# Gate and up products as pairs of 64-row matmuls on two row tiles, with the last 64 rows of K taken out of the seven products

## The chip, the cores and the metric

The kernel runs on one core of one Trainium2 chip. A core has five engines that run at the same time, each with its own queue of instructions worked off in order: TensorE (PE in the profile; its weight loads are listed apart as PEld), VectorE (DVE), ScalarE (ACT), GpSimd (POOL) and SyncE (SP), which here only issues transfers. Engines wait for each other by semaphores. Matrix products go to PSUM, eight banks of 128 partitions by 512 float32 values; everything else lives in SBUF, 128 partitions wide. The metric is device time in microseconds (us).

## The reference

`x` is 2048 tokens by 576 numbers. After a layer norm over the 576 numbers (`xn`), two branches are computed and joined.

```python
s = _A_ref(xn, A_wqkv, A_wo)     # linear attention, 32 heads of 18
def _B_ref(x, w_gate, w_up, w_down):          # B branch, 576 -> 4608 -> 576
    g = jnp.einsum("bsd,df->bsf", x, w_gate)
    u = jnp.einsum("bsd,df->bsf", x, w_up)
    h = _gelu(g) * u
    return jnp.einsum("bsf,fd->bsd", h, w_down)
return x + s * _silu(_B_ref(xn, B_w_gate, B_w_up, B_w_down))
```

The change touches the products by `w_gate` and `w_up`: 576 rows of K, 4608 columns each, 2048 tokens.

## The kernel before

**Words.** All large products are made in the type fp32r with each operand cut into two words: `hi` is the value rounded to fp32r, `lo` the rest. A product is then hi·hi + hi·lo + lo·hi, three matmuls over the same K. ScalarE writes `hi` (a copy), VectorE subtracts to get `lo`.

**Stages.** Normalization and the q, k, v products come first; the tokens turned to operands (`xo`, 128 rows by 5 slots by 512 tokens) are kept. The attention output follows (`s_mm`). Then comes the gate and up stage, 36 matrices of 256 columns (18 groups, each gate and then up), and after it the down products (`down_all`, PSUM tiles `bd`).

**Gate and up.** A Strassen-Winograd scheme works on a two by two split: K into two halves of 288 rows, the tokens into two halves again, the 256 columns of a matrix into two of 128. It needs seven products instead of eight. Each is made for two token sets of 512 (`SBS = (1, 0)`), so a product is two results of 128 columns by 512 tokens. Its left side is a weight block or a sum of blocks (A11, S2, S1, S3, A12, S4, A22, W_AT, line 855), its right side a token block or a difference (B11, T2, T1, T3, B21, B22, T4). The banks are `al`, `be`, `ga`, `de`, one of each for each set; `al`, `ga` and `de` are added to a second time by the fifth to the seventh product.

**One product** (`product`, line 907) is seven matmuls into one bank, by the table PASSES (line 54): 288 rows are two blocks of 128 and a rest of 32. Blocks 0 and 1 take three word pairs each. The seventh pass takes the three word pairs of the rest at once: the rest stands three times in slot 2, 32 rows each, so that 96 of 128 rows carry hi·hi, hi·lo and lo·hi. In all there are 7 products x 2 sets x 7 passes = 98 matmuls to a matrix.

**Around the products** (`matrix`, line 914): after each product VectorE or ScalarE takes its banks. `u` is a copy of `al` by ScalarE; sums with `be`, `ga`, `de` follow on VectorE; in a gate matrix ScalarE applies GELU to the four results as they come (`gate_matrix`, line 1025), in an up matrix VectorE multiplies into them (`up_matrix`, line 1045). The results stand in seventeen places (`spot_h`, `spot_m`, `spot_g`), are summed by GpSimd for the down stage and sent to DRAM (`hs`) by SP.

**The next matrix's weights** are prepared beside this: `load_mat` (line 862) loads the raw block into its one buffer `raw`, `mat_sums` (line 867) makes four block sums on GpSimd, `cut_w` (line 879) cuts words. `mat_pieces` (line 886) says after which product a piece goes: A11 after the first, S2, S1 and S3 after the fourth, A12 and A22 after the fifth, S4 after the sixth. They land in two tiles, `wa` and `wb`. After the last matrix's products stand pieces of the down stage in the same way (`down_first`, line 1306; `cut`, line 1126).

The program order on each engine is the order of the code (`tc.keep_in_program_order`); the waits are found by the framework from the tiles that are read and written.

Of the kernel before, what the change touches and what calls it, by code (L numbers as in the profile page):

```python
# [16 lines left out]
P = 128  # L17
S = 2048
D = 576
DF = 4608  # L20
# [71 lines left out]
SIGN = (-1, 1, -1, -1, 1, -1, 1, 1)  # L92

# [4 lines left out]
def block_kernel(ctx, tc, x, xe, xt, wq_d, wkv_d, wo, wgu_d, wd_d, out):  # L98
# [238 lines left out]
    def difference(s, i):  # L337
        f = xf[s]
        nm, a, b, o = SUMS[i]
        vec("tensor_sub", f[o], f[a], f[b])  # L340
        f[nm] = f[o]

    def keep(s, nm, o):
        d = dr.tile([P, 5, TBN], F32, name=f"kept_{s}_{nm}")
        dma(out=d, in_=o.bitcast(F32))
        store[s, nm] = d

    full = slice(0, TBN)

    def build(s, nm, i):  # L350
        xo[s][nm] = o = big(i, [P, 5, TBN], F32R, f"xo_{s}_{nm}")
        to_operand(o, xf[s][nm], full)
        return o
# [508 lines left out]
    def load_mat(q):  # L862
        if q < NQ:
            raw[q] = mid(0, [P, 2, 3, 2 * P], F32, f"raw_{q}")
            dma(out=raw[q], in_=wgu_d[q // 2, q % 2])

    def mat_sums(q):
        if q >= NQ:
            return
        rv = raw[q].rearrange("p j k (f c) -> p j f k c", f=2)  # L870
        a11, a21, a12, a22 = rv[:, 0, 0], rv[:, 0, 1], rv[:, 1, 0], rv[:, 1, 1]
        sm = mid(2, [P, 4, 3, P], F32, f"sm_{q}")
# [6 lines left out]
    def cut_w(o, src):  # L879

        r = slice(2 * KR, 3 * KR)
        act(o[:, :, 0:3, :], src, AF.Copy)
        vec("tensor_sub", o[:, :, 3:5, :], src[:, :, 0:2, :], o[:, :, 0:2, :].bitcast(F32))
        vec("tensor_sub", o[r, :, 2, :], src[r, :, 2, :], o[r, :, 2, :].bitcast(F32))

    def mat_pieces(q):
# [6 lines left out]
        else:  # L893
# [3 lines left out]
            ]  # L897
        return [
# [8 lines left out]
    def product(o, w, xop, start):  # L907
        for n, (wi, xi, rows) in enumerate(PASSES):
            nc.tensor.matmul(  # L909
                o, w[0:rows, wi, :], xop[0:rows, xi, :],  # L910
                start=(start and n == 0), stop=(n == len(PASSES) - 1), skip_group_check=True,
            )

    def matrix(q, c22, done, todo):

        u, bs = {}, {}

        def both(bk, wn, xn, start):
            for s in SBS:
                if start:  # L920
                    bs[bk, s] = (own_bank if bk == "al" else bank)(f"{bk}_{q}_{s}")
                product(bs[bk, s], w_at(q, wn), X[s][xn], start)

        both("al", "A11", "B11", True)
        for s in SBS:
            u[s] = tmp([P, TBN], f"u_{q}_{s}")
            act(u[s], bs["al", s], AF.Copy)
        run(todo[0])
        both("be", "S2", "T2", True)
        for s in SBS:  # L930
            vec("tensor_add", u[s], u[s], bs["be", s])
        run(todo[1])
        both("ga", "S1", "T1", True)
        for s in SBS:
            vec("tensor_add", c22(s), u[s], bs["ga", s])
        run(todo[2])
        both("de", "S3", "T3", True)
        for s in SBS:
            o = c22(s) if q % 2 == 0 else bs["be", s]
            vec("tensor_add", o, c22(s), bs["de", s])  # L940
            done(s, 1, 1, o)
        run(todo[3])
        both("al", "A12", "B21", False)
        for s in SBS:
            done(s, 0, 0, bs["al", s])
        run(todo[4])
        both("ga", "S4", "B22", False)
        for s in SBS:
            done(s, 0, 1, (u[s], bs["ga", s]))
        run(todo[5])  # L950
        both("de", "A22", "T4", False)
        for s in SBS:
            done(s, 1, 0, (u[s], bs["de", s]))
        run(todo[6])
# [579 lines left out]
    def form_begun(nm):  # L1534

        f = xf[0][nm]
        xo[0][nm] = o = big(12, [P, 5, TBN], F32R, f"xo_0_{nm}")
        act(o[:, 0:3], f, AF.Copy)

        def rest():  # L1540
            r = slice(KR, 2 * KR)
            vec("tensor_sub", o[:, 3:5], f[:, 0:2], o[:, 0:2].bitcast(F32))
# [177 lines left out]
```

## Time and profile before

| what | value |
|---|---|
| median of 3 runs | 1453.61 us (1453.46 to 1453.86) |
| profiled execution, its own time | 1452.58 us |
| span of its profile | 1450.9 us |
| TensorE busy, matmuls | 1444.4 us, 8272 matmuls |
| VectorE busy | 1148.7 us |
| ScalarE busy | 565.2 us |
| GpSimd busy | 580.1 us |
| gate and up stage | from 276.2 to 1076.0 us, 3528 matmuls |

The span is what the profile covers; 1.7 us of the profiled execution lie outside it. Busy time of an engine is the union of its instructions; a matmul's recorded length contains its way through the array, so one matmul's record overlaps the next, and the pace is read from the distance of starts, or from the length of a stretch over the number of its matmuls. In the lines by group the numbers are: count, busy time, mean length of one in ns, idle time of the engine just before them.

### The profile page before, as it was taken

How to read it: one execution, taken by the hardware profiler on the slowest of the kernel's cores; microseconds unless marked ns; L12 is line 12 of the kernel's file. 1: busy time of each engine (PE TensorE's matmuls, PEld its weight loads, DVE VectorE, ACT ScalarE, POOL GpSimd, SP SyncE). 2: the span in 40 equal slices, each digit the busy share in tenths (PEclk: the TensorE clock that was granted, in tenths of full speed). 3: DMA queues.
4: the chain of work that ended last, by engine and by line, in shares of the span. 5: the costliest groups of instructions: out<-in, count | busy, mean ns of one | idle time of the engine just before them, and what ended most of it. 6: DMA issues, size and time to landing. Idle time of an engine off the chain costs nothing.

```text
span 1450.9 us, 22169 instructions
## 1 busy us (share of the span) xinstructions
PE 1444.4 (100%) x8272; PEld 1286.5 (89%) x8272; DVE 1148.7 (79%) x1609; ACT 565.2 (39%) x918; POOL 580.1 (40%) x520
## 2 busy tenths in 40 slices
PE   9999999999999999999999999999999999999998
PEld 8989989988888888888888888888889999999998
DVE  7688666476787887887777878778888978989898
ACT  6444365333222233322332232332235556555454
POOL 3342340225756567566475754667632000000000
PEclk9999999999999999999999999999999999999999
DMA  5554115521532315224242243323379888767886
GB/s 221 186 205 158 45 36 207 224 95 51 171 101 100 131 52 188 88 95 140 72 159 87 97 150 102 117 87 121 126 272 347 269 261 252 249 188 235 278 293 225
DMA packets 119253, 235.04 MB, mean 162 GB/s; under 512 B 11658, under 2 KB 45354, under 8 KB 117226
## 3 DMA queue, kind: packets, MB, share of 16 engines
q1 hardware_dynamic: 116346, 221.37, 45.4%
q0 software_dynamic: 2656, 12.06, 2.2%
q8 instruction: 65, 1.06, 0.3%
q14 instruction: 42, 0.34, 0.1%
q10 hardware_dynamic: 144, 0.20, 0.0%
HBM read 150.96 MB, written 82.58 MB: 161 GB/s over the span
## 4 chain that ended last, share of the span: by engine, by line
PE 97%; DVE 1%; ACT 1%; issue 0%; POOL 0%; DVEq 0%; ACTq 0%; POOLq 0%
PE bd L147 25%; PE al L909 16%; PE ga L909 16%; PE de L909 16%; PE kv L147 8%; PE be L909 8%; PE s L147 4%; PE q L147 3%; PE kv_a L147 1%; PE idle L147 0%; PE d L147 0%; PE kw L147 0%; PE b L147 0%; ACT e_q L141 0%; PE xt L264 0%
## 5 line engine op out<-in xcount | busy, mean ns | idle before, releaser
L150 POOL TENSOR_TENSOR sm<-raw 128x384 f32<-128x384 f32 x72 | 75.0, 1041 | 144.0 <-DMA raw<-in_wgu_dram 125.8
L147 PE MATMUL kv<-wkv,xo_B 128*128 128x412 f32 (+2 forms) x662 | 125.0, 347 | 0.3 <-ACT xo_B L141 0.3
L147 PEld LDWEIGHTS kv<-wkv,xo_B 128*128 128x128 f32 x662 | 120.2, 188 | 1.7 <-ACT xo_B L141 0.9
L144 DVE TENSOR_TENSOR wa<-sm,wa 128x768 fp32r<-128x768 f32 x72 | 90.5, 1257 | 36.0 <-ACT wa L141 35.2
L147 PE MATMUL bd<-w_head,hi 128*128 128x288 f32 x516 | 117.5, 294 | 0.0
L144 DVE TENSOR_TENSOR wb<-raw,wb 128x256 fp32r<-128x256 f32 (+1 forms) x108 | 103.2, 955 | 7.2 <-ACT wb L141 5.5
L144 DVE TENSOR_TENSOR wa<-raw,wa 128x256 fp32r<-128x256 f32 x72 | 66.8, 928 | 50.6 <-ACT wa L141 47.4
L141 ACT ACTIVATE hi<-raw_h 128x1024 fp32r<-128x1024 f32 x59 | 62.5, 1059 | 96.1 <-PE bd L147 55.7
L147 PE MATMUL bd<-w_end,hi 128*128 128x288 f32 x448 | 89.4, 294 | 0.0
L141 ACT ACTIVATE spot_h<-spot_h 128x512 f32<-128x512 f32 x49 | 30.7, 633 | 150.1 <-DVE spot_h L144 150.1
L147 PEld LDWEIGHTS bd<-w_head,hi 128*128 128x128 f32 x516 | 86.8, 188 | 0.1
L144 DVE TENSOR_TENSOR raw_h<-raw_h,hi 128x1024 fp32r<-128x1024 f32 x59 | 71.8, 1221 | 18.8 <-ACT hi L141 18.8
L141 ACT ACTIVATE wa<-sm 128x1152 fp32r<-128x1152 f32 x36 | 41.8, 1161 | 92.8 <-PE de L909 92.8
L147 PE MATMUL bd<-w_end,raw_h 128*128 128x288 f32 x264 | 77.6, 294 | 0.0
L141 ACT ACTIVATE u<-al 128x512 f32<-128x512 f32 x72 | 41.0, 592 | 90.0 <-PE al L909 60.0
L147 PEld LDWEIGHTS bd<-w_end,hi 128*128 128x128 f32 x448 | 71.6, 188 | 0.0
L147 PE MATMUL bd<-beside,raw_h 128*128 128x288 f32 x240 | 70.5, 294 | 0.0
L150 POOL TENSOR_TENSOR spot_h<-spot_h,spot_h 128x512 f32<-128x512 f32 x45 | 62.8, 1403 | 2.9 <-DVE spot_h L144 2.4
L909 PE MATMUL al<-xo_B,wa 128*128 128x512 f32 x252 | 63.0, 389 | 0.0
L909 PE MATMUL al<-xr_B,wa 128*128 128x512 f32 x252 | 63.0, 389 | 0.0
L909 PE MATMUL be<-xo_T,wa 128*128 128x512 f32 x252 | 63.0, 389 | 0.0
L909 PE MATMUL be<-xr_T,wa 128*128 128x512 f32 x252 | 63.0, 389 | 0.0
(278 smaller groups left out, 4036.8 us busy)
## 6 DMA issues: line engine op xcount, KB each, us to landing
raw_h<-hs SPq DMA_DIRECT2D x176, 256.0 KB
raw<-in_wgu_dram SPq DMA_DIRECT2D x36, 768.0 KB
hs<-spot_h SPq DMA_DIRECT2D x90, 256.0 KB
hs<-spot_g SPq DMA_DIRECT2D x80, 256.0 KB
b<-in_wd_dram SPq DMA_DIRECT2D x42, 432.0 KB
hs<-spot_m SPq DMA_DIRECT2D x38, 256.0 KB
raw_g<-hs SPq DMA_DIRECT2D x22, 256.0 KB
raw_a<-hs SPq DMA_DIRECT2D x20, 256.0 KB
```

Source lines behind the costliest of these rows:

```text
L141: pin(nc.scalar.activation(*args, **kw))
L144: pin(getattr(nc.vector, op)(*args, **kw))
L147: pin(nc.tensor.matmul(*args, **kw))
L150: pin(getattr(nc.gpsimd, op)(*args, **kw))
L909: nc.tensor.matmul(o, w[0:rows, wi, :], xop[0:rows, xi, :], start=(start and n == 0), stop=(n == len(PASSES) - 1), skip_group_check=True,)
```

## The change

The last 32 rows of each half of K, 64 rows in all, leave the Strassen scheme. The seven products then cover K as two halves of 256, six passes each (table MAIN: slots 0 and 1 are hi, 2 and 3 of the weight lo). The 64 rows are added to the four results directly: to C22 with the fourth product, to the others with the last three (`tail_of`).

Every pass is made of 64-row matmuls. The array's upper and lower 64 rows are two row tiles. A product now has two phases. In the first (`phase(False, ...)`) rows 0 to 63 of the weight meet token set 1 and rows 64 to 127 meet token set 0, matmul by matmul in turn, each into its set's bank. In the second (`phase(True, ...)`) the sets change rows. The two phases of a product do not follow each other: `step` puts the first phase of the next product between them. After each first phase ScalarE copies one column of set 0's bank to a small tile (`seen`). What followed a product before (`post_0` to `post_6`) now follows, in program order, the first phase of the product two further on.

The 64 rows stand in slot 2 of T1, T3 and T2 as hi in one half of the 128 rows and lo in the other, and as a fifth block of the raw weights, twice (rows 0 to 63 and again 64 to 127); `cut_tail` makes their hi and lo. One such matmul pair belongs to the first phase (hi weight, lo token) and two to the second (hi and lo weight, hi token). `cut_w` no longer cuts a third slot, GpSimd's sums are 256 wide instead of 384, a raw block is 5 x 256 values to a row instead of 6 x 256.

The core of the diff:

```diff
+MAIN = ((0, 0), (0, 2), (2, 0), (1, 1), (1, 3), (3, 1))
+XW = (0, 1, 3, 4)
+TAIL = {"T1": (0,), "T3": (1,), "T2": (0, 1)}
+TR = P // 2
...
     def difference(s, i):
...
-        vec("tensor_sub", f[o], f[a], f[b])
+        vec("tensor_sub", f[o][:, 0:2], f[a][:, 0:2], f[b][:, 0:2])
...
+    def tail(s, nm, o):
+        h = s * TR
+        for j in range(2):
+            vs = [xf[s][BS[b][j]][:, 2, :] for b in TAIL[nm]]
+            r, low = (slice(i + j * KR, i + (j + 1) * KR) for i in (h, TR - h))
+            v = vs[0][r]
+            if len(vs) == 2:
+                d = tmp([P, TBN], f"xd_{s}_{j}")
+                vec("tensor_sub", d[r], v, vs[1][r])
+                v = d[r]
+            act(o[r], v, AF.Copy)
+            vec("tensor_sub", o[low], v, o[r].bitcast(F32))
...
     def cut_w(o, src):
-        r = slice(2 * KR, 3 * KR)
-        act(o[:, :, 0:3, :], src, AF.Copy)
-        vec("tensor_sub", o[:, :, 3:5, :], src[:, :, 0:2, :], o[:, :, 0:2, :].bitcast(F32))
-        vec("tensor_sub", o[r, :, 2, :], src[r, :, 2, :], o[r, :, 2, :].bitcast(F32))
+        act(o[:, :, 0:2, :], src, AF.Copy)
+        vec("tensor_sub", o[:, :, 2:4, :], src, o[:, :, 0:2, :].bitcast(F32))
+
+    def cut_tail(q):
+        o, src = wt["tail", q % 2], raw[q][:, 4, :]
+        act(o[:, 0], src, AF.Copy)
+        vec("tensor_sub", o[:, 1], src, o[:, 0].bitcast(F32))
...
-    def product(o, w, xop, start):
-        for n, (wi, xi, rows) in enumerate(PASSES):
-            nc.tensor.matmul(
-                o, w[0:rows, wi, :], xop[0:rows, xi, :],
-                start=(start and n == 0), stop=(n == len(PASSES) - 1), skip_group_check=True,
-            )
+    def half_passes(rows, o, w, xop, tail_, late):
+        wi = [(w[rows, i, :], xop[rows, XW[k], :]) for i, k in MAIN]
+        if tail_:
+            wt_, xt_ = tail_
+            wi += [(wt_[rows, i, :], xt_[rows]) for i in range(1 + late)]
+        return [(o, a, b) for a, b in wi]
+
+    def phase(late, prod):
+        o, w, xs_, start, tails_ = prod["o"], prod["w"], prod["x"], prod["start"], prod["tail"]
+        pair = []
+        for rows, s in ((LOWER, 0 if late else 1), (UPPER, 1 if late else 0)):
+            pair.append([
+                (s, *p) for p in half_passes(rows, o[s], w, xs_[s], tails_ and tails_[s], late)
+            ])
+        n = len(pair[0])
+        for k in range(n):
+            for side in range(2):
+                s, o_, a, b = pair[side][k]
+                mm(
+                    o_, a, b, start=(start and not late and k == 0), stop=(late and k == n - 1),
+                    skip_group_check=True,
+                )
+
+    def step(prod, post):
+        phase(False, prod)
+        for s in TOUCH:
+            act(seen[:, s : s + 1], prod["o"][s][:, 0:1], AF.Copy)
+        for f in posts[:-1]:
+            f()
+        del posts[:-1]
+        for p in begun_:
+            phase(True, p)
+        begun_[:] = [prod]
+        posts.append(post)
...
+        both("al", "A11", "B11", True, post_0)
+        both("be", "S2", "T2", True, post_1)
+        both("ga", "S1", "T1", True, post_2)
+        both("de", "S3", "T3", True, post_3, tail_of(1, "T3"))
+        both("al", "A12", "B21", False, post_4, tail_of(0, "T1"))
+        both("ga", "S4", "B22", False, post_5, tail_of(0, "T3"))
+        both("de", "A22", "T4", False, post_6, tail_of(1, "T2"))
```

How the change moves instructions is shown at two places. The first is TensorE at the start of matrix 10 (a gate matrix). A name such as `al_10_1` is the bank, the matrix and the token set; `xo_1_B11` and `xr_B11` are block B11 of set 1 and of set 0. Before, seven passes of one set follow each other:

```order
L909 MATMUL al_10_1_4674<-xo_1_B11_1135,wa_2927 128x512 x7
L909 MATMUL al_10_0_4682<-xr_B11_2594,wa_2927 128x512 x7
L909 MATMUL be_10_1_4698<-xo_1_T2_2544,wa_2927 128x512 x7
L909 MATMUL be_10_0_4706<-xr_T2_2686,wa_2927 128x512 x7
L909 MATMUL ga_10_1_4718<-xo_1_T1_2335,wa_2927 128x512 x7
```

Now, with only the first pair of each phase shown (each is repeated five times, and `de_9` has two pairs from the tail behind):

```order
L152 MATMUL al_10_1_5656<-xo_1_B11_1151,wa_2953 128x512 [waits DVE_49]
L152 MATMUL al_10_0_5657<-xr_B11_2621,wa_2953 128x512 [waits DVE_49]
L152 MATMUL de_9_0_5505<-xr_T4_3075,wb_3060 128x512 [waits Activation_49]
L152 MATMUL de_9_1_5504<-xo_1_T4_2709,wb_3060 128x512
L152 MATMUL be_10_1_5693<-xo_1_T2_2564,wa_2953 128x512
L152 MATMUL be_10_0_5694<-xr_T2_2712,wa_2953 128x512
L152 MATMUL al_10_0_5657<-xr_B11_2621,wa_2953 128x512 [waits Activation_49]
L152 MATMUL al_10_1_5656<-xo_1_B11_1151,wa_2953 128x512
```

The two sets alternate matmul by matmul, the second phase of a product stands behind the first phase of the next, and it begins with a wait for ScalarE. The second place is ScalarE from the end of matrix 10 into matrix 11. Before:

```order
L141 ACTIVATE wb_3036<-raw_11_4626 128x384 [waits Activation_49]
L141 ACTIVATE wb_3036<-raw_11_4626 128x384
L141 ACTIVATE spot_h0_3053<-spot_h0_3053 128x512 [waits DVE_49]
L141 ACTIVATE spot_g4_3062<-spot_g4_3062 128x512 [waits DVE_49]
L141 ACTIVATE wb_3036<-sm_11_4669 128x384 [waits PE_49,Activation_49,Pool_49]
L141 ACTIVATE spot_h2_3055<-spot_h2_3055 128x512 [waits DVE_49]
L141 ACTIVATE spot_g0_3058<-spot_g0_3058 128x512 [waits DVE_49]
L141 ACTIVATE u_11_1_4853<-al_11_1_4837 128x512 [waits PE_49]
```

Now:

```order
L146 ACTIVATE wb_3060<-raw_11_5632 128x256 x3
L146 ACTIVATE seen_87<-al_11_0_5919 128x1 [waits PE_49,Activation_49]
L146 ACTIVATE spot_h0_3077<-spot_h0_3077 128x512 [waits DVE_49]
L146 ACTIVATE spot_g4_3086<-spot_g4_3086 128x512 [waits DVE_49]
L146 ACTIVATE wb_3060<-sm_11_5651 128x256 [waits Pool_49]
L146 ACTIVATE seen_87<-be_11_0_5956 128x1 [waits PE_49,Activation_49]
L146 ACTIVATE spot_h2_3079<-spot_h2_3079 128x512 [waits DVE_49]
L146 ACTIVATE spot_g0_3082<-spot_g0_3082 128x512 [waits DVE_49]
L146 ACTIVATE seen_87<-ga_11_0_5987 128x1 [waits PE_49,Activation_49]
```

The one-column copies of matrix 11's first phases now stand between the GELUs of matrix 10's last two products (`spot_...<-spot_...`), and TensorE's second phases wait for these copies.

More of the change, by code (lines that the diff above doesn't have):

```diff
@@ L914, in matrix, with flush @@
+    begun_, posts = [], []
+    def step(prod, post):
[9 more added lines that the diff above has]
+        posts.append(post)
+    def flush():
+        phase(True, begun_.pop())
+        for f in posts:
+            f()
+        posts.clear()
     def matrix(q, c22, done, todo):
@@ L932, in matrix @@
[L932 to L954, printed above, removed]
+        wtail = wt["tail", q % 2]
+        def tail_of(f, nm):
+            c = slice(f * P, (f + 1) * P)
+            return [(wtail[:, :, c], X[s][nm][:, 2, :]) for s in range(2)]
+        def both(bk, wn, xn, start, post, tail_=None):
+            if start:
+                for s in SBS:
+                    bs[bk, s] = (own_bank if bk == "al" else bank)(f"{bk}_{q}_{s}")
+            step({
+                "o": [bs[bk, s] for s in range(2)], "w": w_at(q, wn), "start": start,
+                "x": [X[s][xn] for s in range(2)], "tail": tail_,
+            }, post)
```

125 lines of the change are left out of this document (88 added, 37 removed).

## The prediction

> **What bounds the kernel now.** I read the page first: busy times, then the chain that ended last.
>
> ```profile
> PE 1444.4 (100%) x8272; PEld 1286.5 (89%) x8272; DVE 1148.7 (79%) x1609; ACT 565.2 (39%) x918; POOL 580.1 (40%) x520
> PE 97%; DVE 1%; ACT 1%; issue 0%; POOL 0%; DVEq 0%; ACTq 0%; POOLq 0%
> ```
>
> TensorE is busy over the whole span and makes 97% of the chain. The waits of PE, all of them, say that nothing holds it up:
>
> ```profile
> PE idle L147 <- POOL ident masks.py:199: 1.6, 1, 1.6
> PE kv L147 <- ACT xo_B L141: 0.3, 1, 0.3
> PE bd L147 <- DVE raw_h L144: 0.2, 1, 0.2
> ```
>
> So time can only come from fewer or quicker passes, and any wait that the change adds to PE is paid in full. The stretch of the gate and up matmuls (duration, then PE busy with its count, PEld, clock, DMA), and below it the whole stage before it:
>
> ```profile
> 276.20:1076.00 799.80, 799.67 (x3528) 662.11 (x3528) 1.00 0.35 119
> 0.00:276.00 276.00, 273.94 (x1934) 254.31 (x1935) 196.52 (x400) 134.97 (x296) 85.11 (x112) 1.00 0.42 150
> ```
>
> 799.80 / 3528 = 0.2267 us a pass, at the full clock (1.00), 98 passes and 22.2 us a matrix. The timeline shows the same pace: seven passes start 1.59 us before the next seven.
>
> ```profile
> 633.38 1.75 PE L909 MATMUL al<-xr_B,wa 128*128 128x512 f32 x7
> 634.97 1.75 PE L909 MATMUL be<-xo_T,wa 128*128 128x512 f32 x7
> ```
>
> **The count.** Three products have 12 main pairs, four have 12 and three tail pairs: 84 + 12 = 96 pairs a matrix against 98 passes. Matmuls and weight loads rise from 98 to 192. All hangs on the time T of a pair: the stage takes 36 x 96 x T = 3456 T. It breaks even at 799.8 / 3456 = 0.2314.
>
> **What a pair costs.** No row of the trace shows two row tiles at once. The nearest are column tiles: `d` makes four matmuls of 128 columns beside each other, `xt` is one such matmul after another.
>
> ```profile
> 196.82 0.32 PE L147 MATMUL d<-ph,small 128*32 128x128 f32 x4
> 196.82 1.08 PE L147 MATMUL d<-ph,small 128*32 128x128 f32 x32
> 7.19 0.85 PE L264 MATMUL xt<-ident,x 128*128 128x128 f32 x6
> L147 PEld LDWEIGHTS d<-ph,small 128*32 128x32 f32 x160 | 4.1, 110 | 0.8 <-issue 0.8
> L147 PEld LDWEIGHTS kv_a<-pk,va 128*64 128x64 f32 x256 | 8.8, 135 | 2.7 <-issue 2.1 <-POOL va L150 0.3 <-ACT va L141 0.2
> L909 PEld LDWEIGHTS al<-xo_B,wb 128*128 128x128 f32 x252 | 47.3, 188 | 9.8
> 29.21 0.14 PEld L147 LDWEIGHTS kv_a<-pk,va 128*64 128x64 f32 x2 [0.28 <-issue]
> ```
>
> Four start within 0.32 - 0.275 = some 0.03 us (7 ns or so apart). Eight groups of four last 1.08: with 0.27 for the last group, seven steps of about 0.11 us. `xt` alone: (0.85 - 0.27) / 5, about 0.12. So a group of four costs what one costs, and the skew between tiles is hidden. Row tiles as good as that give T = 0.227. I take this value.
>
> From below: a pass of 288 columns in the down stage,
>
> ```profile
> 1199.96 0.29 PE L147 MATMUL bd<-w_end,raw_h 128*128 128x288 f32 x1
> 1200.09 0.43 PE L147 MATMUL bd<-w_end,beside 128*128 128x288 f32 x2
> 1200.35 0.29 PE L147 MATMUL bd<-w_end,raw_h 128*128 128x288 f32 x1
> 1200.48 0.29 PE L147 MATMUL bd<-w_end,beside 128*128 128x288 f32 x1
> ```
>
> four starts in 0.52, 0.130 each. Then 224 columns cost 0.097, or 0.43 ns each, and 512 columns 0.221. The remaining 6 ns and the uncertainty of the slope (0.41 ns would make it 0.21) are what pairs could hide: T from 0.21.
>
> From above: two 128-column weight loads belong to each pair. If they go one after the other, `bd` bounds them: one load goes with each of its matmuls, so a load takes at most 0.130 and two 0.26. The recorded lengths 110, 135 and 188 for 32, 64 and 128 columns grow by 0.8 ns a column, so the bare load is nearer 0.106 and two in a row 0.212, which still hides under 0.227. In the last row of the fence above two column tiles load together, 0.14 for both against 0.135 for one. That is why I take no cost for the loads.
>
> The Trainium skill (TensorE: Matmul & The Clock Gate, section on LDWEIGHTS) says that a load costs by its columns, whatever the rows; so a 64-row load is no cheaper, which speaks against doubling them. By its formula two take an estimated 0.213, and the sum stays as it is; the growth by columns agrees with the three rows, the rule on rows no run here shows.
>
> Term: 3456 x 0.2267 - 799.8 = **-16.3** (bounds -74 at 0.21, +99 at 0.26).
>
> **The new wait on ScalarE.** Each second phase waits for the one-column copy of its own first phase. It costs some 0.2 us by the smallest copy in the trace, and a second phase starts at least 12 pairs (2.7 us) after its first ended, so as long as ScalarE is on time it is free. But ScalarE works in order, and in gate matrices it is late:
>
> ```profile
> L141 ACT ACTIVATE st<-st 128x2 f32<-128x2 f32 (+1 forms) x10 | 2.0, 203 | 0.3
> 652.42 1.75 PE L909 MATMUL de<-xr_T,wb 128*128 128x512 f32 x7
> 649.69 5.48 DVE L144 TENSOR_TENSOR wb<-raw,wb 128x256 fp32r<-128x256 f32 x4
> 661.20 0.69 DVE L144 TENSOR_TENSOR spot_h<-u,de 128x512 f32<-128x512 f32 x1 [2.16 <-DMA hs<-spot_h]
> 661.92 0.63 ACT L141 ACTIVATE spot_h<-spot_h 128x512 f32<-128x512 f32 x1 [2.21 <-DVE spot_h L144]
> DVE spot_h L144 <- DMA hs<-spot_h: 13.5, 6, 2.4
> DVE spot_g L144 <- DMA hs<-spot_g: 2.9, 1, 2.9
> DVE spot_m L144 <- DMA hs<-spot_m: 2.3, 1, 2.3
> ```
>
> The last product ended at 652.42 + 1.75 = 654.17, its second GELU at 662.55, 8.4 us later: VectorE was held by the cuts of the next weights (5.48), SP's raw load waited for these, the transfers that free the places stood behind it, and the sum for the GELU waited for such a transfer. The last three rows count such waits: 8, against 18 gate matrices. Before, this cost PE nothing. Now the copy of the next matrix's third product stands behind that GELU, and PE wants it 6+6+6+6+7 = 31 pairs, 7.0 us, after the gate matrix's last phase. Unchanged lateness: 8.4 + 0.2 - 7.0 = 1.6 us, eight times: 13 us. It should shrink, since VectorE loses the 32-row cuts:
>
> ```profile
> L144 DVE TENSOR_TENSOR wa<-sm,wa 32x384 fp32r<-32x384 f32 x35 | 43.1, 1231 | 0.8
> L144 DVE TENSOR_TENSOR wa<-raw,wa 32x128 fp32r<-32x128 f32 x35 | 36.3, 1038 | 1.1
> L144 DVE TENSOR_TENSOR wb<-raw,wb 32x128 fp32r<-32x128 f32 x36 | 28.1, 781 | 0.5
> L144 DVE TENSOR_TENSOR wb<-sm,wb 32x128 fp32r<-32x128 f32 x36 | 19.2, 533 | 0.5
> L144 DVE TENSOR_TENSOR wb<-raw,wb 32x256 fp32r<-32x256 f32 x18 | 15.5, 860 | 0.3
> ```
>
> 142 us of VectorE go in the stage; back comes one 128x256 cut a matrix. That time itself is off the path. Of the 5.48 I expect an estimated 1.2 to go (two of four instructions leave, one comes; the raw load is five sixths as long). Left are 0.4 us eight times: **+3** (bounds 0 and 13).
>
> The tightest bank is `al`: the next matrix's first phase overwrites it, and the two GELUs that read it stand behind the one-column copy of the seventh product's first phase. Between that phase and the overwriting lie eight pairs, 1.81 us.
>
> ```profile
> L141 ACT ACTIVATE spot_h<-al 128x512 f32<-128x512 f32 x23 | 13.4, 589 | 3.4 <-PE al L909 3.4
> ```
>
> The drain of 0.16 (1.75 for seven passes, less 7 x 0.2267), the copy and two GELUs make 1.54: some 0.25 to spare, so I count nothing.
>
> **The exit.** In the down stage VectorE's cuts are wanted early:
>
> ```profile
> 1075.90 1.22 DVE L144 TENSOR_TENSOR raw_a<-raw_a,hi 128x1024 fp32r<-128x1024 f32 x1
> 1076.06 0.42 PE L147 MATMUL bd<-w_head,hi 128*128 128x288 f32 x2
> 1077.03 0.69 DVE L144 TENSOR_TENSOR de<-u,de 128x512 f32<-128x512 f32 x1
> 1079.69 1.85 DVE L144 TENSOR_TENSOR raw_b<-raw_b,beside 128x1024 fp32r<-128x1024 f32 x1
> ```
>
> Before, the cut for `bd`'s second unit ended at 1077.1, 2 us ahead of its use (a unit of 24 matmuls takes 3.1). Now the sixth product ends only eight pairs before `bd` starts instead of 14 passes, and VectorE's queue is some 3 us later: **+2** (0 to 3).
>
> **Elsewhere.** Building T1, T3, T2 takes per token set some 14 small instructions on 32 rows more and the old third slot less; PE fills 273.9 of the first 276 us, and the small pieces hide under it: **+0.5** (-1 to 2).
>
> **Sum**, against the profiled execution (1452.58, of which 1450.9 span): -16.3 + 3 + 2 + 0.5 = -10.8, so 1441.8. The median of the runs stands 1.0 above that execution: **1443**.
>
> **Rivals.**
> A pair hides the gap between passes, too (T = 0.217, the middle of 0.21 and 0.221 rounded): 750 for the stage, -50 + 8 (ScalarE comes nearer the edge): about 1411. For it: one tile can stream while the other changes weights. Against: each tile has its own change of weights, and `d` gains nothing over `xt`.
> The skew is not hidden (T = 0.227 + 0.007): 807.7, +8 + 5.5: about 1467. Against it stands that `d` hides it. The Trainium skill (same page, measured speedup of packing) counts about 4 ns for each further tile on top of one matmul; an estimated 0.231 would give no change.
> The weight loads go in sequence, T = 0.247 to 0.26 (slower; decides from 0.2314 on): +54 to +99 and 5.5: 1513 to 1558.
> T as forecast, but ScalarE's lateness bites at its upper bound or in more phases (slower from 16.7 us on): -16.3 + 16 to 22 + 2.5: 1456 to 1462.
> The row tiles do not run side by side at all: 6912 x 0.2267 = 1567, about 2220. Only that no row shows them speaks for it.
>
> **Chances.** Forecast 0.44, own range 1436 to 1451; gap hidden 0.16; skew 0.10; loads 0.15; ScalarE 0.10; no overlap 0.05. 0.2% or 2.9 us is what can be told from no change. Faster: the forecast but 0.02 of it, and the hidden gap, 0.58; same: that 0.02, half of ScalarE, 0.02 of the skew, 0.09; slower: the rest, 0.33. The range 1402 to 1512 leaves out the last rival, most of the serial loads and a little of the hidden gap.
>
> **What would show it.** Starts of one tile 0.227 apart, the other tile's 7 ns behind, confirm the pair; 0.26 means the loads. The waits of PE should list `seen` on ScalarE, single waits under 2 us and some eight of them; more, or over 10 us in all, means that the fourth rival was priced too low. PE waits for VectorE's `raw_a`, `raw_b` behind the stage's end show the exit. The prediction falls with T outside 0.224 to 0.231.

## The result: 2.6% slower, and the profile after

The changed kernel takes 1492.01 us (1491.05 to 1492.34 in four runs) for 1453.53 before: ratio 1.0264, 95% interval 1.0246 to 1.0282. The profiled execution took 1491.87, of which 1490.0 are span, 39.1 more than before. The page of the changed kernel, busy times and then the chain that ended last:

```profile
PE 1462.9 (98%) x11656; PEld 1406.8 (94%) x11656; DVE 998.5 (67%) x1491; ACT 575.3 (39%) x1217; POOL 515.7 (35%) x520
PE 91%; DVE 4%; DMA 3%; ACT 1%; issue 1%; SPq 0%; DVEq 0%; ACTq 0%
```

VectorE is busy for 150 us less; the prediction had counted 142 out and one short cut a matrix back. TensorE is busy for 18.5 us more, although 96 pairs stand for 98 passes, and makes 91% of the chain for 97%. The main waits of PE in the changed kernel (in all, how often, longest), none of which was over 0.3 before; the list has smaller ones, and the 1.6 of `idle` as before:

```profile
PE bd L152 <- ACT hi L146: 8.5, 1, 8.5
PE kv L152 <- ACT xo_B L146: 4.3, 1, 4.3
PE ga L152 <- DVE spot_m L149: 2.7, 1, 2.7
PE al L152 <- DMA xr_B<-kept_B: 1.6, 1, 1.6
PE b L152 <- ACT s L146: 0.9, 1, 0.9
PE de L152 <- DVE spot_g L149: 0.5, 1, 0.5
```

No row of that list names `seen`: the copies that PE was to wait for are never late enough to show. The stretches ahead of the stage, the stage, the gap behind it and the down products (columns as in the prediction):

```profile
0.00:289.50 289.50, 281.26 (x1936) 258.77 (x1936) 198.02 (x406) 138.69 (x307) 83.00 (x113) 0.98 0.39 138
289.50:1099.40 809.90, 804.99 (x6914) 773.21 (x6912) 461.24 (x693) 237.26 (x668) 411.55 (x382) 1.00 0.31 107
1099.40:1108.10 8.70, 0.29 (x3) 0.00 (x0) 1.36 (x1) 2.19 (x2) 0.00 (x0) 0.63 0.89 302
1108.10:1485.70 377.60, 376.21 (x2808) 374.84 (x2808) 336.91 (x389) 196.80 (x240) 21.14 (x26) 0.99 0.82 263
```

All four are longer than before. The table has them for every kernel of this study, from the starts of matmuls in the traces: the first of the stage ("front"), the stage from its first start to its last, from there to the first of `bd`, `bd` from first to last. The last column is the time; `after` and e10 were timed four times, the experiments beside them once. Single runs of the kernel before, taken beside the experiments, lie between 1452.6 and 1454.8, so a difference of one or two us between two times says little by itself; there the traces are read.

| kernel | front | stage | gap | bd | time |
|---|---|---|---|---|---|
| before | 276.3 | 799.5 | 0.2 | 370.3 | 1453.5 |
| after | 289.6 | 809.7 | 8.9 | 377.4 | 1492.0 |
| e1 | 286.9 | 799.4 | 9.1 | 374.6 | 1476.1 |
| e3 | 289.8 | 812.9 | 2.6 | 379.5 | 1491.0 |
| e4 | 285.7 | 810.1 | 9.1 | 376.9 | 1489.0 |
| e5 (e1 and more) | 285.5 | 801.3 | 0.3 | 373.5 | 1466.9 |
| e6 (e5 and more) | 285.8 | 787.3 | 0.3 | 373.0 | 1452.6 |
| e7 (e6 and more) | 277.1 | 787.3 | 0.3 | 372.2 | 1443.4 |
| e10 (e7 and more) | 277.2 | 784.7 | 0.3 | 372.7 | 1441.2 |
| e2 (before, 8 bytes) | 278.1 | 816.3 | 0.2 | 374.6 | 1475.5 |
| e8 (before, 32 bytes) | 278.3 | 816.3 | 0.2 | 373.8 | 1474.8 |
| e9 (before, 64 bytes) | 277.8 | 817.5 | 0.2 | 373.8 | 1475.6 |
| e11 (before, 128 bytes) | 277.7 | 817.0 | 0.2 | 373.4 | 1474.6 |
| e12 (before, weights moved) | 276.4 | 823.0 | 0.2 | 370.8 | 1476.7 |

So of the 39.2 us (these starts leave out little at the ends) the front took 13.3, the stage 10.2, the exit 8.7 for the gap and 7.1 in `bd`. All these kernels compute the whole reference.

### The profile page after: what moved, and what is told of

The parts are those of the page before. It is cut to its first block, busy times and chain, and to the rows that moved or that the text cites. A ratio compares the mean times of both kernels' runs of the same rounds, so it can differ in the third digit from the quotient of the medians.

```text
span 1490.0 us, 29114 instructions
## 1 busy us (share of the span) xinstructions
PE 1462.9 (98%) x11656; PEld 1406.8 (94%) x11656; DVE 998.5 (67%) x1491; ACT 575.3 (39%) x1217; POOL 515.7 (35%) x520
## 4 chain that ended last, share of the span: by engine, by line
PE 91%; DVE 4%; DMA 3%; ACT 1%; issue 1%; SPq 0%; DVEq 0%; ACTq 0%
PE bd L152 22%; PE de L152 16%; PE al L152 15%; PE ga L152 15%; PE kv L152 8%; PE be L152 6%; PE s L152 4%; PE q L152 2%; DMA raw_h<-hs 1%; PE kv_a L152 1%; DVE xo_T L149 1%; DMA xr_B<-kept_B 1%; DVE wa L149 0%; DMA raw_a<-hs 0%; DMA hs<-spot_g 0%
## 5 line engine op out<-in xcount | busy, mean ns | idle before, releaser
L152 PE MATMUL de<-xo_T,wa 64*128 64x512 f32 x540 | 144.4, 393 | 0.0
L152 PE MATMUL de<-xr_T,wb 64*128 64x512 f32 x540 | 142.8, 392 | 0.0
L152 PE MATMUL de<-xr_T,wa 64*128 64x512 f32 x540 | 142.0, 390 | 0.5 <-DVE spot_g L149 0.5
L152 PE MATMUL de<-xo_T,wb 64*128 64x512 f32 x540 | 140.6, 388 | 0.0
L152 PE MATMUL ga<-xo_T,wa 64*128 64x512 f32 x486 | 130.9, 393 | 0.0
L152 PE MATMUL ga<-xr_T,wa 64*128 64x512 f32 x486 | 130.7, 393 | 0.0
L152 PE MATMUL al<-xr_B,wb 64*128 64x512 f32 x432 | 113.2, 395 | 1.6 <-DMA xr_B<-kept_B 1.6
L152 PE MATMUL al<-xo_B,wb 64*128 64x512 f32 x432 | 113.2, 394 | 0.0
L152 PE MATMUL ga<-xr_B,wb 64*128 64x512 f32 x432 | 113.1, 394 | 0.1
L152 PE MATMUL be<-xo_T,wa 64*128 64x512 f32 x432 | 112.2, 392 | 0.0
```

What stands on the lines that cost most here:

```text
L152: pin(nc.tensor.matmul(*args, **kw))
```

## Experiments

### The pace of a pair: e1, e2, e8, e9, e11, e12

In the changed kernel's stage, starts on a row tile that lie more than 330 ns apart cost 8.4 us beyond a pair's pace. Without these 8.4 the 3456 pairs take 801.3, or 0.232 each, where the prediction had 0.2267. But 0.232 is only an average: by their tiles, some groups run as forecast and others do not (matmuls of the stage, two groups of each kind: count, busy time, mean ns of one, idle before):

```profile
L152 PE MATMUL al<-xr_B,wa 64*128 64x512 f32 x432 | 110.5, 388 | 0.0
L152 PE MATMUL de<-xo_T,wb 64*128 64x512 f32 x540 | 140.6, 388 | 0.0
L152 PE MATMUL be<-xr_T,wa 64*128 64x512 f32 x432 | 112.1, 392 | 0.0
L152 PE MATMUL be<-xo_T,wa 64*128 64x512 f32 x432 | 112.2, 392 | 0.0
```

In the quick groups starts on one row tile are mostly 226 or 227 ns apart (T3 of set 0, which runs beside slow groups, averages 230), in the others mainly 232 and 235 in turn, and the difference goes with the X block alone, not with the bank, the weight or the row tile. The quick blocks are the five (B11 of both sets, T3 of set 0, B22 and T4 of set 1) that the allocation places behind the new tile `seen`; both weight tiles lie there too. The other nine lie ahead of it. The tile has 8 bytes, and tiles start at multiples of 32, so it moved what follows it by 32 bytes against what precedes it. (Places are read from the allocation; no trace prints an address.) That was to be tested both ways: take it out of the change, and put it into the kernel before.

```diff
+    spare = eps_t[:, 8:10]            # e1, in the changed kernel
     eps_t, zx = eps_t[:, 0:1], eps_t[:, 2:3]
...
-    seen = sb.tile([P, 2], F32, name="seen")
+    seen = spare
```

> The changed kernel, but the one-column copies go into two spare columns of a tile that was there before; the 8-byte tile of their own is gone, and every tile placed behind it (both weight tiles, five of the X blocks) lies 8 bytes lower. Nothing else is different. Theory A (the pace of a pass hangs on where weights and X lie in relation to each other: the blocks placed behind the small tile ran at 226.7 ns, those placed ahead of it at 231.7 and 235.0 in turn): all blocks run at 226.7, the stage of the gate and up matmuls falls from 809.7 to about 792 and the time from 1492 to about 1474. Rival B (64-row passes, the new layout of the weights or the other row tile's weight loads cost the 6.7 ns): the slow blocks stay slow, the time stays within 3 of 1492.

```diff
+    seen = sb.tile([P, 2], F32, name="seen")     # e2, in the kernel before
+    pool("memset", seen, 0.0)
     def product(o, w, xop, start):
```

> The kernel before with the 8-byte tile added at the same place in the code and written once; nothing reads it. Theory A (addresses): the blocks placed ahead of it get a pass of about 233 ns for 227, in some two thirds of 3528 passes, so the stage rises from 799.8 by about 15 to 18 and the time to about 1470. Rival B (row tiles or the new weight layout): no change, 1453.5 within 1.5.

e1 took 1476.1, 15.9 less, and e2 1475.5, 22.2 more than before. In e1 the slow groups are quick, and all starts of a row tile but those over 330 ns average 226.8 ns:

```profile
L152 PE MATMUL be<-xr_T,wa 64*128 64x512 f32 x432 | 109.4, 386 | 0.0
L152 PE MATMUL be<-xo_T,wa 64*128 64x512 f32 x432 | 109.4, 386 | 0.0
```

In e2, matmuls of 128 rows, with one row tile and the old weight layout, split into the same five quick blocks, at 389 to 392 (the first passes behind a slow block still lag), and nine others at 395 and 396; the two of each kind as above:

```profile
L912 PE MATMUL al<-xr_B,wa 128*128 128x512 f32 x252 | 63.0, 389 | 0.0
L912 PE MATMUL de<-xo_T,wb 128*128 128x512 f32 x252 | 63.2, 390 | 0.0
L912 PE MATMUL be<-xr_T,wa 128*128 128x512 f32 x252 | 64.7, 396 | 0.0
L912 PE MATMUL be<-xo_T,wa 128*128 128x512 f32 x252 | 64.7, 396 | 0.0
```

Row tiles have no part in it: rival B falls. e1's stage missed its 792 by 7, which the section on waits takes up. The 2.7 that e1 won in the front go with the addresses, too: 1.0 of it stands in the 512-column passes of `q`, 229.4 ns apart for 234.3 in the changed kernel. The rest is spread over other matmuls and waits. Left were which distances are slow, and whether weights and X are what stands at a distance. e8, e9 and e11 are e2 with tiles of other sizes:

```diff
+    seen = sb.tile([P, 8], F32, name="seen")     # e8; e9: [P, 16]; e11: [P, 32]
```

> The kernel before with a tile of 32 bytes in the place where e2_before_plus_8_bytes had one of 8 (which gave 1475.5 for 1453.2, with twelve of the fourteen X blocks at up to 233.6 ns a pass). Nothing reads it. Which distances between the weights and the X blocks are slow is not known. Theory A1 (the distance counts modulo 64 bytes or more): the same blocks are slow, about 1470 to 1476. Theory A2 (modulo 32 bytes or less): no change, 1453.5 within 1.5.

> As e8, with 64 bytes. Theory A1a (modulo 128 bytes or more): slow, 1470 to 1476. Theory A1b or A2 (modulo 64 or less): no change, 1453.5 within 1.5.

> As e2, e8 and e9, with a tile of 128 bytes. By the allocation, tiles start at multiples of 32 bytes, so the 8 bytes of e2 moved what lies behind them by 32, as e8 did; in the kernel before, the weights and all X blocks start at multiples of 256. Theory A1 (the distance between weights and X counts modulo 256 bytes): nine blocks at 233, 1470 to 1476. Theory A2 (modulo 128): no change, 1453 within 1.5.

They took 1474.8, 1475.6 and 1474.6. (That of e8 says twelve of fourteen blocks; it was nine.) By the allocation, all X blocks and weights of the kernel before start at multiples of 256 bytes, some at an odd one: 256 between them is quick, 32, 64 and 128 are slow. e12 moves the weights alone:

```diff
-        wt["a"] = big(15, [P, 4, 5, P], F32R, "wa")       # wt["b"] likewise
+        wt["a"] = big(15, [P, 16 + 20 * P], F32R, "wa")[:, 16:].rearrange(
+            "p (f k c) -> p f k c", f=4, k=5)
```

> The kernel before, with the two weight tiles begun 64 bytes into their places; no other tile moves. Theory A (the distance between the weights and the X block of a pass): now all fourteen X blocks are at a wrong distance, all 3528 passes at about 233.3, the stage 823 for 799.5, the time about 1477. Rival (what counts is where something else lies that e2, e8 and e9 had moved with the weights, or the X blocks' own addresses): no change, 1453 within 1.5.

It took 1476.7, with a stage of 823.0 for the 823 expected. The stretch of the stage in e12 (all passes, clock 1.00), and two of its fourteen groups, which all read 395 or 396:

```profile
276.30:1099.50 823.20, 823.20 (x3530) 663.32 (x3530) 617.72 (x824) 235.55 (x384) 473.93 (x382) 1.00 0.34 116
```

```profile
L909 PE MATMUL al<-xr_B,wa 128*128 128x512 f32 x252 | 64.5, 395 | 0.0
L909 PE MATMUL be<-xo_T,wa 128*128 128x512 f32 x252 | 64.7, 396 | 0.0
```

So it is the distance between the weights and the X block of a pass: at a multiple of 256 bytes a pass takes 226.7 ns, at the others tried 233. The `bd` matmuls gain or lose with the tiles' places too: their starts are 131.7 ns apart before, in e12, where their tiles stayed, and in e1, but 133.0 in e2 and in the changed kernel. The column `bd` shows it, with 370.3 before, 370.8 in e12, and 373.4 to 374.6 in e2, e8, e9 and e11.

### The exit: e3 and e5

In the changed kernel, the SP queue at the stage's end, and ScalarE's first cut for `bd`:

```profile
1099.50 0.37 SPq L158 DMA_DIRECT2D b<-in_wd_dram  x1
1099.97 2.35 SPq L158 DMA_DIRECT2D raw_a<-hs  x4
```

```profile
1099.73 1.16 ACT L146 ACTIVATE w_end<-b 128x1152 fp32r<-128x1152 f32 x1 [3.44 <-PE de L152]
1107.08 1.06 ACT L146 ACTIVATE hi<-raw_a 128x1024 fp32r<-128x1024 f32 x1 [6.18 <-DMA raw_a<-hs]
```

and the same loads in the kernel before, 9.3 us ahead of the first `bd` at 1076.06:

```profile
1066.78 1.76 SPq L153 DMA_DIRECT2D raw_a<-hs  x4
```

The loads stand behind one part of the down weights (`b`, "42"), which goes to the place of T2 of set 0. T2 used to be read for the last time in the second product. Now its third slot holds the tail that the seventh product reads. e3 moves that load behind the others.

```diff
-            [lambda: load_reg("42", "42")],      # step 1 of down_first
+            [],
...
-            [],
+            [lambda: load_reg("42", "42")],      # step 6
```

> The changed kernel, but the load of one part of the down weights into the place of block T2 (which must wait for the last product's tail) is issued three steps later, behind the loads for the first down matmuls on SP's queue instead of ahead of them. Theory: those loads stand behind a wait that ends only at the last read of T2; with that gone the 8.5 us wait of the first down matmul goes, and the slow clock behind it: down 12 to 15, to about 1478. Rival (VectorE or ScalarE being late by the shifted phases makes the wait): under 4 us of gain, the wait of the first down matmul stays over 5.

1491.0: 1 us gained for 12 to 15. Neither theory nor rival came out: the wait did fall, to 2.2, but the time hardly did. The gap fell to 2.6 but `bd` grew by 2.1, and the stage, by waits and slow pairs in other places, by 3.1. The row of `w_end` above says why: its place is T2 of set 1, so the first down words wait for the last product as well. e5 takes the cause away instead of one of its victims: the tail goes to T4, whose third slot was empty.

```diff
-TAIL = {"T1": (0,), "T3": (1,), "T2": (0, 1)}
+TAIL = {"T1": (0,), "T3": (1,), "T4": (0, 1)}
...
-        both("de", "A22", "T4", False, post_6, tail_of(1, "T2"))
+        both("de", "A22", "T4", False, post_6, tail_of(1, "T4"))
...
-        for i, nm_ in enumerate((nm, "T2")):       # kept(0, "T2") below likewise
+        for i, nm_ in enumerate((nm, "T4")):
...
+            lambda: open_block(1, "T3", X_SLOT["T3"]), lambda: open_block(1, "T4", X_SLOT["T4"]),
```

(`open_block` takes the place and makes the tail, ahead of the rest of the block.)

> e1_seen_moved (1476.1), and the tail that belongs to the last product lies in the third slot of T4, which that product reads anyway and which was empty, and no longer in T2's. So both T2 blocks come free after the second product, as before the change. For the second token set the tails of T3 and T4 are made three steps earlier, ahead of the first raw load that waits for their source. Theory (two things waited for the last read of T2: the down weights in its place for set 0, with the first down loads behind them on SP, and the first down weight words in its place for set 1, which is why the experiment with the later load won only 4.2 us at the exit): the first bd matmul starts 0.2 to 1 us behind the stage's last start instead of 9, the slow clock behind the gap goes, exit 10 to 13 shorter; and the raw load that waited on SP for T2's tail at 243.8 goes at about 230, so that the stage starts 3 to 6 earlier. Time about 1460. Rival (the exit is late because VectorE and ScalarE get the last sums two phases later): the gap at bd stays over 4, the time over 1468.

1466.9, 9.2 under e1. In e5's SP queue the loads are back ahead of `bd`, which starts at 1087.14, 0.3 behind the stage:

```profile
1078.18 2.09 SPq L158 DMA_DIRECT2D raw_a<-hs  x4
```

Against e1 the gap and `bd` are 9.8 shorter, a little under the 10 to 13 expected, while the stage is 2.0 longer, mostly by slow pairs behind the wait for B21. With the first `bd` right behind the stage, the tail in T2 is shown as what held up the exit. At the front the guess was too high: the raw load went at 239.9 for the 230 expected, and the stage started 1.4 earlier, not 3 to 6.

### Waits inside the stage: e6

With the pace back, eight waits show at bank `de`, one in each two groups; by the starts of pairs they cost 0.6 to 1.8 us each, 6.7 in all. In the changed kernel the slower pace had hidden most of them. PE's waits inside the stage in e1, and three of VectorE's there:

```profile
PE de L152 <- DVE spot_h L149: 3.4, 6, 0.8
PE ga L152 <- DVE spot_m L149: 3.2, 1, 3.2
PE de L152 <- DVE spot_g L149: 1.6, 1, 1.6
PE de L152 <- DVE spot_m L149: 0.4, 1, 0.4
PE al L152 <- DMA xr_B<-kept_B: 1.9, 1, 1.9
```

```profile
DVE spot_h L149 <- DMA hs<-spot_h: 16.7, 6, 3.0
DVE spot_g L149 <- DMA hs<-spot_g: 3.6, 1, 3.6
DVE spot_m L149 <- DMA hs<-spot_m: 2.9, 1, 2.9
```

These are the eight late sums that the prediction counted under ScalarE, by VectorE's waits for stores of `hs`. They are no longer free. The bank `de` is overwritten 24 pairs, 5.4 us, after its last product; before it was 42 passes, 9.5 us. The wait at `ga` begins at VectorE, in the changed kernel at 1057 (and, not shown, at 1044 in e1):

```profile
1057.18 7.20 DVE L149 TENSOR_TENSOR wa<-raw,wa 128x256 fp32r<-128x256 f32 x1 [2.99 <-ACT wa L146]
1064.31 1.27 DVE L149 TENSOR_TENSOR u<-u,be 128x512 f32<-128x512 f32 x2
```

```profile
1057.24 1.30 POOL L155 TENSOR_TENSOR spot_h<-spot_h,spot_h 128x512 f32<-128x512 f32 x1
1062.80 1.29 POOL L155 TENSOR_TENSOR spot_h<-spot_h,spot_g 128x512 f32<-128x512 f32 x1
```

This subtraction of 256 columns takes 7.20 while GpSimd goes without a pause through five additions and a DMA issue, from 1057.24 to 1064.09 (the first and the last addition are shown). The trace has 144 such cuts of weights: 110 take at most 0.45, and only five of these lie beside sums of GpSimd at all; 33 take 0.5 to 1.6 and this one 7.20, and each of these 34 lies beside GpSimd's sums for at least four fifths of its time. So a cut is slow where GpSimd is adding; why this one outlasted five additions, where the others outlast one or two, is open. Before, this cut came at another moment of GpSimd's work. PE's wait then costs two thirds as much again: for some 4 us the starts of pairs are up to 427 ns apart, and the profile gives the clock of that stretch as 0.67 (PE busy, clock, DMA):

```profile
1066.90:1072.00 5.10, 5.10 (x32) 0.67 0.34 129
```

e6 makes four changes of order and none of work:

```diff
-            [lambda: cut_w(wt["a"][:, 0:1], rv[:, 0, 0:1])],     # mat_pieces: step 0
             [], [],
+            [lambda: cut_w(wt["a"][:, 0:1], rv[:, 0, 0:1])],     # step 2
...
-        eng = nc.gpsimd if m == NM - 1 else nc.sync
+        eng = nc.gpsimd if m == NM - 1 and at >= HOOKS * m + 20 else nc.sync
...
-    load_mat(1)
+    load_mat(1, nc.gpsimd)
...
-        todo[4].append(lambda q=q: load_mat(q + 2))     # ahead of run_events
+        todo[4].append(lambda q=q: load_mat(q + 2))     # behind run_events
```

> e5, and three changes of order against the waits inside the stage: the load of the next raw weights stands behind the stores of that step on SP's queue (it blocked them, and one of them frees the place that the sum of the last product's bank waits for); the first cut of the next matrix comes two steps later; the first stores of the last group of hidden sums go by SP instead of GpSimd; and the second raw load of the start goes by GpSimd's queue, so that block B21 comes first on SP's. Theory: the eight waits of about 0.9 at bank de (7 in all), the 3.8 at ga with the slow pairs behind it (2.5) and the 2.3 for B21 go: the stage takes 784 to 787 for 799, the time is 10 to 14 under e5. Rival (the shorter distance between a bank's last read and its next use, 24 pairs or 5.4 us for 42 passes or 9.5, is met by VectorE whatever SP does): the waits at de stay, under 6 of gain.

1452.6, 14.3 under e5; the stage takes 787.3. The whole list of PE's waits in e6 inside the stage is one row, and VectorE waits for no store any more:

```profile
PE al L152 <- DMA xr_B<-kept_B: 1.9, 1, 1.9
```

The waits at `de` and `ga` came from the order of work, and the rival (VectorE meets the shorter distance whatever SP does) falls. The four edits were not tried apart: that the load's new place on SP freed `de`, and which edit freed the 7.2 us subtraction, is argued. B21's wait stayed: that edit won nothing.

### The front: e4 and e7

VectorE in the changed kernel while the tail of T2 is made (the rest of each 1.4 us it waits for ScalarE):

```profile
98.90 0.68 DVE L149 TENSOR_TENSOR xd<-xf_B,xf_B 32x512 f32<-32x512 f32 x1
100.28 0.68 DVE L149 TENSOR_TENSOR xo_T<-xd,xo_T 32x512 fp32r<-32x512 f32 x1 [0.70 <-ACT xo_T L146]
100.99 0.68 DVE L149 TENSOR_TENSOR xd<-xf_B,xf_B 32x512 f32<-32x512 f32 x1
102.37 0.68 DVE L149 TENSOR_TENSOR xo_T<-xd,xo_T 32x512 fp32r<-32x512 f32 x1 [0.70 <-ACT xo_T L146]
103.08 0.69 DVE L149 TENSOR_SCALAR ph<-q 128x512 f32<-128x512 f32 x1
```

32 rows cost what 128 cost. VectorE comes to the statistics of the next tokens at 111.76, before at 106.37, and PE waits 4.3 for the tokens. e4 gives these instructions to GpSimd and makes the two halves together:

```diff
-            act(o[r], v, AF.Copy)                  # tail(): half by half
-            vec("tensor_sub", o[low], v, o[r].bitcast(F32))
+        for (r, low), v in zip(rs, vs):            # behind both differences, by pool as well
+            act(o[r], v, AF.Copy)
+        for (r, low), v in zip(rs, vs):
+            pool("tensor_sub", o[low], v, o[r].bitcast(F32))
```

> The changed kernel, but the 64-row tails of T1, T3 and T2 are built in three steps for both halves (all differences, all high parts, all low parts), and differences and low parts by GpSimd instead of VectorE. Theory: the small instructions that wait for ScalarE and back hold up VectorE by some 5 us at each of two places and all behind it; with them away the stage of the gate and up matmuls starts at 276 to 279 for 289.6, and the time falls by 10 to 13, to about 1480. Rival (the later raw load and GpSimd's or the DMA queues' order make the front late, not VectorE): the stage still starts after 285; GpSimd, which then has the work, may make it later still.

1489.0: 3 us for 10 to 13. The stage started at 285.7, after 285 as the rival had it, and the wait of `kv` grew:

```profile
PE kv L152 <- ACT xo_B L146: 5.4, 2, 5.1
```

GpSimd takes 1.3 to 1.5 us for each, and ScalarE and then VectorE wait for it. That leaves open whether VectorE's share of the work made the front late; e7 takes the work away instead of moving it. It can be dropped at two of three places: T1's and T3's tails are rows whose `hi` and `lo` already stand in the third slots of the token blocks, and DMA moves them; only T4's tail is a difference.

```diff
+        if len(TAIL[nm]) == 1:                     # tail(), here and below
+            for j in range(2):
+                src = xo[s][BS[TAIL[nm][0]][j]]
+                for k, at_ in ((0, h), (1, TR - h)):
+                    dma(out=o[at_ + j * KR : at_ + (j + 1) * KR].bitcast(F32),
+                        in_=src[k * KR : (k + 1) * KR, 2, :].bitcast(F32))
+            return
```

> e6, and the 64-row tails of T1 and T3 are no longer computed: their high and low parts stand in the third slots of the token blocks already and are moved by DMA, 32 rows each; only the tail of T4, a difference, is computed, in three steps (differences, high parts, low parts). VectorE loses 5.4 us of small instructions ahead of the gate and up matmuls, and the waits for ScalarE between them. Theory (the front is late since each of these 32-row instructions costs VectorE as much as one of 128 rows, 0.68): the wait of the key and value matmuls for ScalarE at 115 (4.3) goes or falls under 1, the stage starts at 276 to 279, 6 to 10 earlier than in e6. Rival (the eight added DMAs a set on SP's queue hold up the loads behind them): the stage starts no earlier than in e6.

1443.4, 9.3 under e6, of which 8.6 lie in the front (277.1) and 0.8 in `bd`. PE's wait of `kv` falls under 1 as expected, so for these 8.6 the tails as they were computed made the front late:

```profile
PE kv L152 <- ACT xo_B L146: 0.7, 1, 0.7
```

### What is left at the start of the stage: e10

A product's first phase comes early: in e1 block B21 is wanted 9.9 us into the stage (296.8 for a start at 286.9), before the change it was 14.3 (290.66 for 276.33). The transfers that share its time are the same.

```diff
-    load_mat(1, nc.gpsimd)
-    back("B21", "B22", "T4", eng=nc.sync)
+    back("B21", eng=nc.sync)
+    load_mat(1)
+    back("B22", "T4", eng=nc.sync)
```

> e7_tails_by_dma (1443.4), but block B21 is fetched first on SP's queue, the second raw weights behind it on the same queue and no longer beside it on GpSimd's. Theory (the three transfers share the DMA engines, and B21, needed 10 us into the stage where it was needed 14 us into it before, comes last): the wait of 2.0 at al and the slow pairs behind it (1.9) go, about 1439.5. Rival (B21's own megabyte and T3's fill the time whatever comes behind them): the wait stays over 1.5, 1442 to 1444.

1441.2 (1440.9 to 1441.4), ratio to the kernel before 0.9919, interval 0.9903 to 0.9936: 0.8% faster than the kernel before. Against e7 the time alone would say little, but in the trace the wait at `al` fell from 2.0 to 0.4, the slow pairs behind it are gone, and the stage is 2.6 shorter; the time came 1.7 over the 1439.5 expected. Its stage, its waits over 0.4 but that of `idle`, and what is left at `al`:

```profile
277.10:1062.20 785.10, 784.39 (x6914) 782.43 (x6912) 456.71 (x695) 241.05 (x671) 407.33 (x376) 1.00 0.32 114
```

```profile
PE bd L152 <- DVE raw_b L149: 1.0, 1, 1.0
PE kv L152 <- ACT xo_B L146: 0.6, 1, 0.6
PE al L152 <- DMA xr_B<-kept_B: 0.4, 1, 0.4
```

## Why the prediction was wrong

The forecast was 1443 and faster; the change gave 1492 and is slower. The range of 1402 to 1512 held it by luck, through none of its rivals: the unhidden skew names nearly the pace that was found, 0.234 for 0.232, and is not its cause.

**The count and the pair (-16.3, found +1.8).** 96 pairs for 98 passes, side by side at the price of one pass: that step was right. From 40 us into e10's stage on, every 40 us average 226.7 ns a pair, two weight loads and all. The change also shows what the prediction could not: a weight load of 64 rows and 128 columns takes 184 ns by its record, one of 128 rows 188, so half the rows save next to nothing, and two to a pair hide even so. What failed is that T was worked out as if the change did nothing else to a matmul. The 8 bytes of `seen` moved weights against X blocks, and 0.2319 for 0.2267 lies just past the 0.231 at which the prediction said it would fall, and past the 0.2314 at which it had the gain end. e1 gives back 17.4 of the 18.1 (the stage without its waits: 801.3 and 783.9). One working on the way does not come out of its own figures: 0.32 less 0.275 is 0.045, not 0.03. The 7 ns that it led to are right all the same, for the trace has the starts of those four column tiles 6 to 7 ns apart.

**The new wait on ScalarE (+3, found 0 in the change).** No run's list of waits names `seen`. The lateness it was built on is real, but it strikes elsewhere: the step "the tightest bank is `al`" failed. `de` is tighter, since its eight late reads are VectorE's, and 24 pairs now stand where 42 passes stood. In e1, with the pace right, they cost 6.7. The bound of 13 covers that, but at the wrong bank.

**The exit (+2, found +15.8).** Some 3 of it are the addresses again: e1 takes `bd` from 377.4 to 374.6. Most of the rest is a reader that was left out. The term asked how late VectorE would be; it did not ask for the tail, which moved the last read of T2 from the second product to the seventh, with two down weight places behind it and SP's queue behind one of these. With both gone (e5 and on), what is left is close to the term itself: gap and `bd` of e10 are 2.4 over before, and its one wait over 0.6 in `bd` is the predicted one for `raw_b`.

**Elsewhere (+0.5, found +13.3).** Here too 2.7 are the addresses (e1), and 1.4 went with the tail's new place (e5). For the 8.6 that e7 took away, "the small pieces hide under it" failed twice: 32-row pieces are not small on VectorE, and what hides under PE's 273.9 busy microseconds is only what no later step waits for. e7 leaves +0.8, so the bound of 2 would have held for a tail without computing.

**No term at all** was there for the 7.2 us subtraction with its slow pairs (5.1 of the stage) and for B21 (1.8): both come from steps that moved in time while their queues kept their order.

With the five causes out, e10's terms against before are -14.8 for the stage, +2.4 for the exit and +0.9 for the front, -11.4 of span in all with 0.1 at the end, for -16.3 + 3, +2 and +0.5, -10.8, predicted. The count and the price of a pair were sound, and the change as it was made loses by what it moved along with it. That the sums lie so close owes something to luck: the 3 for ScalarE never came, and 1.5 of other waits stand in the stage in their place. The repairs had little to win in the kernel before, whose waits of PE are 2.1 in all.

## What to carry to other kernels

After a change, compare where the operands of the hot loop lie and not only the instructions: a tile of 8 bytes cost 16 to 22 us here, and groups by tile with one mean above the others showed it at once. When a block is read later than before, list every load and word that waits for its place, and for every bank the distance from the last read to the next write. Small instructions on few rows are priced like large ones, so count them; on a queue in order, look at what is issued behind a wait before giving the work to another engine.

## What the runs showed of the hardware

**Distance of the operands.** Passes of 512 columns at 226.7 ns when weights and moving operand start a multiple of 256 bytes apart by the allocation, on average 232 to 234 at 32, 64 or 128 bytes off (e1, e2, e8, e9, e11, e12). The Trainium skill (SBUF — State Buffer, section on who interferes with whom) says that TensorE reads its moving operand and its weights by two independent ports and never waits on anyone; e12, where only the weights moved, measures 3% against that, and the measurement decides. Why 256, and what lies between the distances tried, is open.

**Row tiles drift.** The two matmuls of a pair do not start together: the upper tile runs 163 ns behind the lower in e10, 223 in e1 and 298 in the change (medians), over a pass late there. In e10 the pace does not suffer: 226.7 ns a pair. The prediction had 7 ns.

**Slow pairs behind a wait.** Where a wait put two starts of a row tile 3.4 to 3.8 us apart, pairs ran at up to 427 ns behind it, and the trace's record of the clock has 0.5 there, for 3.41 us or twice that. At about 2 us between starts it went either way (2.05 in e3 and 2.31 in e5 were followed by slow pairs, 1.95 in the change and 2.31 in e1 were not). The Trainium skill (TensorE: Matmul & The Clock Gate, section on what is actually happening) has the clock at half after an idle window of some 3.4 us that runs free. The half clock and the 3.41 us agree; that 2.05 us from start to start can be enough does not fit an idle window of that length, and here the measurement decides.

**VectorE beside GpSimd.** Of 144 cuts of weights of 256 columns in the changed kernel, with both inputs in SBUF, the 34 that took over 0.45 us all lie beside GpSimd's sums, and 105 of the other 110 do not. The longest, 7.20 us, outlasted five additions and a DMA issue. That GpSimd holds them up rests on this coincidence in time; no run took GpSimd's work away by itself.
